# A third pair of score blocks on VectorE in every second head group of an attention kernel

## The chip, the cores and the metric

The kernel runs on one core of a Trainium2 chip. The metric is the device time of one execution in microseconds (us), lower is better. Each kernel was run several times next to the kernel before, on the same chip. A profile shows one execution. Its engines are PE (TensorE; PEld is its weight loads), ACT (ScalarE), DVE (VectorE), POOL (GpSimd) and SP (the queue that issues most transfers, 541 of 601). The granted clock is the share of its full clock that TensorE was given. "L497" is line 497 of the kernel's file; the changed kernel has one line more, so lines after 513 are one higher there.

## The reference, cut to what matters

```python
def _A_ref(x, wqkv, wo):                      # x: 1 x 2048 x 512, 32 heads of 16
    q, k, v = split(x @ wqkv)
    scores = einsum("bhqd,bhkd->bhqk", q, k) * Dh ** -0.5
    p = softmax(scores)                       # 32 x 2048 x 2048 exponentials
    return einsum("bhqk,bhkd->bhqd", p, v) -> heads joined @ wo
def _B_ref(q, k, v, shift_k, ssm_k, ssm_D):   # a causal convolution of length 2048 per channel, 512 channels
    ...
return concatenate([a, b], axis=-1)
```

The 134 million exponentials of the softmax are the part that matters. The convolution runs in the background: its matmuls fill PE's time between the attention's, and 268 MB of shifted filter rows (tile WR) are loaded for it.

## The kernel before

The scores come in blocks of 128 keys x 512 queries. A head group (four heads, 512 queries) has 64 blocks. There are 32 groups, 0 to 31; groups 4 to 31 are the steady part. PE works in steps of three blocks, 21.3 steps to a group:

```python
for T in range(NT + 3):          # NT = 692 steps
    emit_qk(T)                   # PE: 3 score matmuls into 3 PSUM banks; ACT: one exponential over them
    emit_pv(...)                 # PE: weighted sums of blocks whose exponentials are done
    emit_bg(T)                   # PE: a slice of the convolution or of a projection, through PSUM bank 7
    if dve_fill and (bank_free == before or dve_fill[0][0] <= T):
        dve_fill.pop(0)[1]()     # DVE: one piece of a pair's exponential
    ...                          # DVE: pieces that end a group (transposes, division)
```

Two sets of three PSUM banks alternate, so the score matmuls of step T+2 overwrite the banks of step T and wait until these have been read (in the trace before, 304 waits for ACT's reading, 119.7 us). DVE and ACT work through their queues in order: in the trace before all DVE operations (804) and all 698 operations of ACT start in the order of the program, compared by line and tile. PE takes the matmuls of a step in the order of the loop above as well (score matmuls, weighted sums, background; seen step by step in the trace before from 400 to 417 us, where in one step two background matmuls stand among the weighted sums), so a score matmul that waits for its bank holds up what follows it.

Exponentials are split between two engines. In most steps ACT takes all three blocks, 1536 columns. In four steps of a group the third block goes to DVE and ACT takes 1024 columns. DVE does two such blocks together, a pair, with bit arithmetic and a polynomial:

```python
DVE_AT = ((3, 5), (12, 14))      # two pairs in each group: the steps that hand over their third block
DVE_LAG = 8

def exp_on_dve(b, bank, h, T):   # shortened
    # "conversion": reads the PSUM bank and so frees it for the score matmuls of step T + 2
    h_fix[i] = dve.op(tensor_scalar(EI[:, i % 2, :], PS[:, bank, :], FIX_LO, FIX_ADD, max, add),
                      [h, h_pair.get(p - 1)])
    def split():                 # mantissa to EM, power of two to EI
        dve.op(tensor_scalar(EM, EI, 0x7fffff, 0x3f800000, and, or))
        dve.op(tensor_scalar(EI, EI, 0x7f800000, 0x40000000, and, xor))
    def horner(j):               # EH = (EH + B) * m, three times; polynomial of degree 4 in m
        dve.op(scalar_tensor_tensor(EH, src, (B3, B2, B1)[j], m, add, mult))
    def last():                  # PTD = (EH + B0) * power of two
        dve.op(scalar_tensor_tensor(PTD, EH, B0, EI, add, mult))
    if i % 2:                    # after the second block of the pair
        dve_fill.extend([split, horner 0, horner 1, horner 2, last])   # one piece a step, as above
```

DVE also evacuates the background's results from bank 7 (YB, QN, QT, OUTA), and PE's next background matmul waits for that.

The softmax here doesn't subtract the row's maximum and nothing guards it: scores larger than these inputs give would overflow.

Of the kernel before, what the change touches and what calls it, by code (L numbers as in the profile page):

```python
# [6 lines left out]
ALU = mybir.AluOpType  # L7
BF16 = mybir.dt.bfloat16
FP32 = mybir.dt.float32
INT32 = mybir.dt.int32  # L10
# [5 lines left out]
QB = 512  # L16
NQB = S // QB
# [9 lines left out]
LKZ = PAD + S  # L27
R_W = 12
R_PT = 4
R_O = 16  # L30
R_A = 4
CHB = 32
PVB = 6
# [8 lines left out]
B0, B1, B2, B3 = 37.6797618003151, 23.053950042922654, 12.310574509367148, -0.15702561410827162  # L42
OCT = 2.0 ** 23
QSCALE = SCALE * math.log2(math.e) * OCT
FIX_LO = -118.0 * OCT
FIX_ADD = (math.log2(C4) - 1.0) * OCT
DVE_AT = ((3, 5), (12, 14))
DVE_LAG = 8
PACE = 3.9

# [43 lines left out]
def bass_concat_heads__mha_block__ssm_conv_h3__prompt_kernel(  # L94
# [17 lines left out]
    def enter(cm):  # L112
        ctxs.append(cm)
        return cm.__enter__()

    def sem(name):
        return enter(nc.semaphore(name))

    def sb(name, shape, dt=BF16):
        return enter(nc.sbuf_tensor(name, shape, dt))  # L120
# [11 lines left out]
    WKV = sb("WKV", [128, 2, 4, D])  # L132
    OTN = sb("OTN", [128, R_O, QB])
    DT = sb("DT", [128, QB], FP32)
# [4 lines left out]
    IDN = sb("IDN", [128, 128])  # L139
    SHK = sb("SHK", [128, 4, 4])  # L140
    PTD = sb("PTD", [128, 2, QB])
    EI = sb("EI", [128, 2, QB], INT32)
    EM = sb("EM", [128, 2, QB], INT32)
    EH = sb("EH", [128, 2, QB], FP32)
    JNK = sb("JNK", [128, 2], FP32)
# [15 lines left out]
    PS = enter(nc.psum_tensor("PS", [128, 8, 512], FP32))  # L161


    pe, act, dve, pool, sp = [Eng(sem(n)) for n in ("s_pe", "s_act", "s_dve", "s_pool", "s_sp")]
# [191 lines left out]
    def unit(u, bank, eng=None):  # L356
        if u[0] == "x":
            turn_x(u[1], u[2], bank, dve)
        elif u[0] == "t":
            spread_tap(u[1], bank)  # L360
        else:
            evac_unit(u, bank, pe_unit(u, bank), eng)
# [65 lines left out]
    chunks = []  # L428
    b_ = 0
    while b_ < NBLK:  # L430
        T = len(chunks)
        n = 2 if (T % 2 == 1 and T < N_EARLY) else 3
        n = min(n, NBLK - b_)
        chunks.append((list(range(b_, b_ + n)), [3 * (T % 2) + i for i in range(n)]))
        b_ += n
    NT = len(chunks)
# [29 lines left out]
    dve_pv = {}  # L466
    for n in range(2, NQB * NG):
        t0 = chunk_of[first[n]][0]
        if t0 < N_EARLY + 30:
            continue  # L470
        for pair in DVE_AT:
            for t in pair:
                on_dve[chunks[t0 + t][0][2]] = len(on_dve)
                dve_pv[chunks[t0 + t][0][2]] = t0 + pair[1] + DVE_LAG

    h_exp = {}
    h_blk = {}
# [28 lines left out]
    h_fix = {}  # L506
    h_ptd = {}
    h_pair = {}

    def exp_on_dve(b, bank, h, T):  # L510
        i = on_dve[b]
        p = i // 2
        m = EM[:, :, :].bitcast(FP32)
        st = {}
        h_fix[i] = dve.op(lambda e: e.tensor_scalar(EI[:, i % 2, :], PS[:, bank, :], FIX_LO, FIX_ADD, ALU.max, ALU.add),  # L515
                          [h, h_pair.get(p - 1)])

        def split():
            st["m"] = dve.op(lambda e: e.tensor_scalar(EM[:, :, :], EI[:, :, :], 0x7fffff, 0x3f800000,  # L519
                                                       ALU.bitwise_and, ALU.bitwise_or), [h_fix[i], h_fix[i - 1]])  # L520
            st["e"] = dve.op(lambda e: e.tensor_scalar(EI[:, :, :], EI[:, :, :], 0x7f800000, 0x40000000,  # L521
                                                       ALU.bitwise_and, ALU.bitwise_xor), [st["m"]])

        def horner(j):
            src = m if j == 0 else EH[:, :, :]
            st["h"] = dve.op(lambda e: e.scalar_tensor_tensor(EH[:, :, :], src, (B3, B2, B1)[j], m, ALU.add, ALU.mult),  # L526
                             [st["m"], st.get("h")])

        def last():
            h_pair[p] = h_blk[b] = h_blk[b1] = dve.op(  # L530
                lambda e: e.scalar_tensor_tensor(PTD[:, :, :], EH[:, :, :], B0, EI[:, :, :].bitcast(FP32),  # L531
                                                 ALU.add, ALU.mult), [st["h"], st["e"], h_ptd.get(p - 1)])
        if i % 2:
            b1 = blk_on_dve[i - 1]
            dve_fill.extend(zip(range(T + DVE_LAG - 6, T + DVE_LAG - 1),
                                [split, lambda: horner(0), lambda: horner(1), lambda: horner(2), last]))
        return h_fix[i]
# [2 lines left out]
    dve_fill = []  # L540

    def oslot(n):
        return (n + 12) % R_O

    h_otn = {}
    dve_later = []
# [31 lines left out]
    def finish_group(n, h, T):  # L578
# [16 lines left out]
        def turn_back(i0, i1):  # L595
            sl = slice(128 * i0, 128 * i1)
            h_otn[(n, i1)] = h_otn[n] = dve.op(
                lambda e: e.transpose(out=OTN[:, oslot(n), sl], in_=dtn[:, sl]),  # L598
                [st["h"], h_wqp[7]] + ([h_op[((n - R_O) // NG, t)] for t in range(4)] if n >= R_O else []))
        if last:  # L600
# [56 lines left out]
    def load_wr(d):  # L657
        r = d % R_W
        deps = [h_kzw[0], h_kvc[0]] if d < R_W else [h_wrfree[d - R_W]]
        src = bass.AP(tensor=kz_ap.tensor, offset=kz_ap[d, 0].offset, ap=[[1, 128], [1, S]])  # L660
        h_wr[d] = dma(sp, d_wr[r], WR[:, r, :], src, deps)

    def load_qn(i, deps):
        h_qn[i] = dma(pool, d_q[i % 2], QN[:, i % 2, :, :],
                      q2[:, 128 * i:128 * i + 128].rearrange("(t p) d -> p t d", p=128), deps)
# [70 lines left out]
    def now(T):  # L736
        t1 = N_EARLY + 30
        return 12.0 + 1.36 * min(T, t1) + 1.28 * max(T - t1, 0)

    def group_step(qb, g):  # L740
        return NT * (qb * NG + g) // (NQB * NG)

    def unit_job(u):
        return [lambda: pe_unit(u, BGB, (0, 1)), lambda: evac_unit(u, BGB, pe_unit(u, BGB, (2, 3)))]
# [5 lines left out]
    def start_job(job):  # L750
        state["gap"] += 1
        state["job"] = job
        state["job"].pop(0)()

    def emit_bg(T):
        st = state
        if not kv_pieces and not st["started"]:
            st["started"] = True
            st["dma"] = now(T) + 18.0
            for i in range(R_W // 4):  # L760
                st["wr"].append(st["dma"] + 1.5)
            for d in range(R_W):
                load_wr(d)
            for i in range(2):
                load_qn(i, [h_kvc[0], h_kzt[0]])
        if T <= max(early):
            if T in early:
                unit(early[T], 5 if T < N_EARLY - 1 else 7)
            return
        if T == max(early) + 1:  # L770
            load_wop(pe_last())
        if st["turn"]:
            conv_turn(st["qd"] // 8 - 1)
            st["turn"] = False
            st["gap"] = 0
            return
        if not st["started"]:
            return
        st["lags"] = min(st["lags"] + PACE, 4.0 * LAGS)
        if st["job"]:  # L780
            st["job"].pop(0)()
            return
        if st["qd"] % 4 == 0 and st["lag"] == 0:
            ready = st["qd"] < C // 4 and st["wr"][st["qd"]] <= now(T)
            jobs = []
            if st["op"] < len(later_op) and (later_op[st["op"]][0] * NG + NG - 1) in h_otn:
                u = later_op[st["op"]]
                jobs.append((NT * (u[0] + 2) // NQB, "op", op_job, u))
            if st["q"] < len(later_q) and T >= group_step(later_q[st["q"]][1] - 2, later_q[st["q"]][2]) + 30:
                u = later_q[st["q"]]  # L790
                jobs.append((group_step(u[1], u[2]), "q", lambda *u: unit_job(u), u))
            if jobs:
                due, kind, make, u = min(jobs, key=lambda j: j[0])
                if st["gap"] < 1 or T + 60 > due or not ready:
                    start_job(make(*u))
                    st[kind] += 1
                    return
        left = min(LAGS, int(st["lags"]))
        while left and st["qd"] < C // 4 and st["wr"][st["qd"]] <= now(T) and not st["turn"]:
            n0 = st["lag"]  # L800
            n1 = min(n0 + left, NB)
            left -= n1 - n0
            st["lags"] -= n1 - n0
            conv_lags(st["qd"], n0, n1)
            st["lag"] = n1 % NB
            if n1 == NB:
                st["qd"] += 1
                for i in range(4):
                    st["dma"] = max(st["dma"], now(T) + 3.0) + 1.42
                st["wr"].append(st["dma"] + 1.5)  # L810
                if st["qd"] % 4 == 0:
                    st["gap"] = 0
                    st["turn"] = st["qd"] % 8 == 0
                    break

    def pe_last():
        return (pe.sem, pe.n)
# [3 lines left out]
    for b in range(NBLK):  # L821
        qb, g, kt, s = blk(b)
        n = qb * NG + g
        t = dve_pv[b] if b in on_dve else chunk_of[b][0] + 2
        if n >= 2:
            t = max(t, chunk_of[last_blk[n - 1]][0] + 3)
# [31 lines left out]
    for t in range(4):  # L858
        h = op_mm(qb, t, 7, 8, banks[t])
# [55 lines left out]
```

## Time and profile before

| | kernel before |
|---|---|
| time, median of the first 3 runs | 926.25 us |
| span of the profiled run | 927.0 us |
| busy: ACT, PE, DVE | 96%, 81%, 68% |
| exponentials on ACT | 552 of 1536 columns, 140 of 1024 |
| blocks on DVE | 112 (28 groups x 4) |

The first view is the page's part 1, busy time of each engine with its share of the span, and part 4, the chain of waits that ended last.

```profile
...
PE 748.9 (81%) x12846; PEld 337.1 (36%) x12892; DVE 634.9 (68%) x804; ACT 892.2 (96%) x699; POOL 47.0 (5%) x65
...
ACT 67%; PE 16%; DMA 7%; DVE 7%; issue 1%; SPq 1%; ACTq 0%
...
```

ACT is the limit: 96% busy and 67% of the chain.

The groups of instructions by form (line, engine, operation, tiles, shapes, count | busy us, mean ns of one | idle time before them and what ended it) give the costs. First ACT:

```profile
...
L497 ACT ACTIVATE PT<-PS 128x1536 bf16<-128x1536 f32 x552 | 788.6, 1632 | 13.9 <-PE PS L490 13.1
L497 ACT ACTIVATE PT<-PS 128x1024 bf16<-128x1024 f32 x140 | 163.8, 1170 | 3.4 <-PE PS L490 3.4
...
```

These durations overlap, so a mean of 1632 ns is not what one costs. From start to start the median is 1.331 us for the long form and 0.904 us for the short one. A block of 512 columns is therefore worth 0.427 us of ACT, 0.834 ns per column. With these two pitches the exponentials of a group in the steady part take 26.72 us on average; I call that the pure time. Groups 4 to 31 took 27.89 us each, 1.17 us more. I call that the excess.

Then the operations of a pair on DVE:

```profile
...
L526 DVE SCALAR_TENSOR_TENSOR EH<-EH,EM 128x1024 f32<-128x1024 f32 x112 | 142.1, 1269 | 3.4
L515 DVE TENSOR_SCALAR EI<-PS 128x512 int32<-128x512 f32 x112 | 78.6, 702 | 90.8 <-PE PS L490 89.9
L526 DVE SCALAR_TENSOR_TENSOR EH<-EM 128x1024 f32<-128x1024 f32 x56 | 71.3, 1273 | 0.0
L531 DVE SCALAR_TENSOR_TENSOR PTD<-EH,EI 128x1024 bf16<-128x1024 f32 x56 | 69.9, 1248 | 1.8
L519 DVE TENSOR_SCALAR EM<-EI 128x1024 int32<-128x1024 int32 x56 | 40.2, 717 | 1.6
L521 DVE TENSOR_SCALAR EI<-EI 128x1024 int32<-128x1024 int32 x56 | 39.8, 710 | 1.9
...
```

A pair is two of L515 and one each of L519 and L521, three of L526 and one of L531: about 7.8 us, once overlaps are taken off.

Waits (who waited for whom: us in all, times, longest):

```profile
...
DVE EI L515 <- PE PS L490: 89.9, 88, 3.1
...
ACT PT L497 <- PE PS L490: 16.5, 34, 2.4
...
```

DVE waits 90 us for scores to convert, so it is ahead, and ACT waits only 16.5 us for scores. No wait of the score matmuls for the conversion is in the list.

The last view is the timeline of DVE alone (start us, duration us, instruction, and in brackets the idle time before it) in group 9, an odd group, whose first pair runs here:

```profile
...
277.63 0.67 DVE L515 TENSOR_SCALAR EI<-PS 128x512 int32<-128x512 f32 x1
...
279.78 0.70 DVE L515 TENSOR_SCALAR EI<-PS 128x512 int32<-128x512 f32 x1
...
283.11 2.70 DVE L526 SCALAR_TENSOR_TENSOR EH<-EH,EM 128x1024 f32<-128x1024 f32 x2
285.85 1.23 DVE L531 SCALAR_TENSOR_TENSOR PTD<-EH,EI 128x1024 bf16<-128x1024 f32 x1
...
288.78 0.69 DVE L515 TENSOR_SCALAR EI<-PS 128x512 int32<-128x512 f32 x1 [0.25 <-PE PS L490]
...
291.79 0.88 DVE L515 TENSOR_SCALAR EI<-PS 128x512 int32<-128x512 f32 x1
...
```

The first pair is finished at 287.1, and the next conversion, at 288.78, finds DVE idle, waiting for PE.

### The profile page before, as it was taken

What the parts mean: (1) busy time and instruction counts of PE and PEld (TensorE: products, weight loads), DVE (VectorE), ACT (ScalarE), POOL (GpSimd) and SP (SyncE); (2) the same over time, 40 slices, a digit from 0 to 9 for tenths busy, and PEclk for the clock granted to TensorE, in tenths of its full rate; (3) what the DMA queues carried; (4) which work ended last, traced back from release to release, by engine and by line L of the source; (5) the groups of instructions that cost most, each with busy time, mean ns of one, the idle gap of its engine ahead of it and who ended that gap; (6) DMA issues with size and microseconds to landing.
All of it is one profiled execution on the core that took longest, in us unless ns stands there. A gap on an engine that the chain in (4) does not pass through costs nothing.

```text
span 927.0 us, 28312 instructions
## 1 busy us (share of the span) xinstructions
PE 748.9 (81%) x12846; PEld 337.1 (36%) x12892; DVE 634.9 (68%) x804; ACT 892.2 (96%) x699; POOL 47.0 (5%) x65
## 2 busy tenths in 40 slices
PE   7998787887777878877777778888778877778887
PEld 3332233433333433333343333333334333333432
DVE  4789627767667756677676577677677677667764
ACT  5999999999999999999999899999999999999995
POOL 2113130000000100000000000000000000000000
PEclk9999999999999999999999899999999999999987
DMA  9643569999999999989999999996999999997741
GB/s 312 232 143 114 155 227 393 335 382 354 373 337 384 362 368 373 341 329 352 386 361 368 330 392 334 353 344 238 375 394 348 394 336 385 346 377 317 297 166 46
DMA packets 88570, 295.59 MB, mean 319 GB/s; under 512 B 11269, under 2 KB 19458, under 8 KB 88066
## 3 DMA queue, kind: packets, MB, share of 16 engines
q1 hardware_dynamic: 82114, 280.13, 81.0%
q0 software_dynamic: 3936, 12.58, 4.2%
q8 instruction: 102, 1.67, 0.7%
q10 hardware_dynamic: 2400, 1.05, 0.4%
q14 instruction: 18, 0.15, 0.0%
HBM read 287.31 MB, written 6.42 MB: 317 GB/s over the span
## 4 chain that ended last, share of the span: by engine, by line
ACT 67%; PE 16%; DMA 7%; DVE 7%; issue 1%; SPq 1%; ACTq 0%
ACT PT L497 67%; DMA WR<-kz_scratch 6%; PE PS L490 4%; PE PS L562 3%; PE PS L678 3%; PE PS L630 2%; PE PS L310 1%; SPq L171 1%; DMA WKV<-in_A_wqkv_dram 1%; PE PS L296 1%; DVE WR L374 1%; DVE WR L378 1%; PE PS L303 1%; DVE EH L526 1%; DVE KTo L333 1%
## 5 line engine op out<-in xcount | busy, mean ns | idle before, releaser
L497 ACT ACTIVATE PT<-PS 128x1536 bf16<-128x1536 f32 (+1 forms) x692 | 886.9, 1539 | 17.3 <-PE PS L490 16.5
L490 PE MATMUL PS<-QT,KTo 32*128 32x512 bf16 x2048 | 277.0, 394 | 128.8 <-ACT PT L497 119.7
L678 PE MATMUL PS<-WR,KV 128*2 128x128 bf16 (+15 forms) x8192 | 306.3, 228 | 18.6 <-DMA WR<-kz_scratch 12.3
L562 PE MATMUL PS<-PT,VAF 128*32 128x512 bf16 x1936 | 295.1, 399 | 2.1 <-DVE DT L584 1.3
L678 PEld LDWEIGHTS PS<-WR,KV 128*14 128x14 bf16 (+15 forms) x8192 | 195.8, 107 | 52.4 <-issue 36.4
L490 PEld LDWEIGHTS PS<-QT,KTo 32*128 32x128 bf16 x2048 | 67.6, 91 | 291.4 <-ACT PT L497 241.0
L526 DVE SCALAR_TENSOR_TENSOR EH<-EH,EM 128x1024 f32<-128x1024 f32 x112 | 142.1, 1269 | 3.4
L515 DVE TENSOR_SCALAR EI<-PS 128x512 int32<-128x512 f32 x112 | 78.6, 702 | 90.8 <-PE PS L490 89.9
L562 PEld LDWEIGHTS PS<-PT,VAF 128*32 128x32 bf16 x1936 | 69.0, 93 | 151.6 <-issue 140.1
L584 DVE STREAM_TRANSPOSE DT<-PS 128x512 f32<-128x512 f32 x31 | 22.2, 717 | 100.1 <-PE PS L562 100.1
L526 DVE SCALAR_TENSOR_TENSOR EH<-EM 128x1024 f32<-128x1024 f32 x56 | 71.3, 1273 | 0.0
L531 DVE SCALAR_TENSOR_TENSOR PTD<-EH,EI 128x1024 bf16<-128x1024 f32 x56 | 69.9, 1248 | 1.8
L519 DVE TENSOR_SCALAR EM<-EI 128x1024 int32<-128x1024 int32 x56 | 40.2, 717 | 1.6
L521 DVE TENSOR_SCALAR EI<-EI 128x1024 int32<-128x1024 int32 x56 | 39.8, 710 | 1.9
L296 PE MATMUL PS<-xT,WQP 128*128 128x512 bf16 x105 | 32.1, 382 | 9.6 <-DVE QN L714 3.2
L630 PE MATMUL PS<-WKV,OTN 128*128 128x512 bf16 x117 | 32.6, 389 | 3.6 <-DVE YB L694 1.2
L324 DVE TENSOR_SCALAR QT<-PS 128x512 bf16<-128x512 f32 x32 | 22.1, 690 | 19.5 <-PE PS L296 19.5
L694 DVE CAST YB<-PS 128x512 bf16<-128x512 f32 x32 | 21.9, 685 | 14.6 <-PE PS L562 12.5
L562 PE MATMUL PS<-PTD,VAF 128*32 128x512 bf16 x112 | 23.5, 417 | 3.4 <-DVE PTD L531 3.3
L171 POOL DMA_DIRECT2D out_dram<-QN x4 | 4.7, 1179 | 405.9 <-DVE QN L714 405.9
L598 DVE STREAM_TRANSPOSE OTN<-DTN 128x512 bf16<-128x512 bf16 (+1 forms) x35 | 23.0, 664 | 0.7
L171 POOL DMA_DIRECT2D out_dram<-OUTA x12 | 6.6, 550 | 332.6 <-DVE OUTA L638 309.8
(62 smaller groups left out, 262.8 us busy)
## 6 DMA issues: line engine op xcount, KB each, us to landing
WR<-kz_scratch SPq DMA_DIRECT2D x512, 512.0 KB, 8.2
WR<-in_B_k_dram POOLq DMA_DIRECT2D x16, 256.0 KB, 4.5
kz_scratch<-WR SPq DMA_DIRECT2D x1, 2176.0 KB, 9.0
KV<-in_A_x_dram SPq DMA_DIRECT2D x4, 512.0 KB, 6.7
QN<-in_B_q_dram POOLq DMA_DIRECT2D x4, 512.0 KB, 11.0
out_dram<-QN POOLq DMA_DIRECT2D x4, 512.0 KB, 8.4
WR<-in_B_v_dram SPq DMA_DIRECT2D x6, 256.0 KB, 2.7
QT<-in_B_k_dram POOLq DMA_DIRECT2D x6, 256.0 KB, 4.8
```

What stands on the lines that cost most here:

```text
L296: return e.matmul(PS[:, bank, :], lhsT=WQP[:, dc, g, :], rhs=xT[:, dc, qb * 512:(qb + 1) * 512], start=(dc == 0), stop=(dc == 3))
L490: ins = e.matmul(PS[:, bank, :], lhsT=KTo[32 * s:32 * s + 32, g // 2, kt * 128:(kt + 1) * 128], rhs=QT[32 * s:32 * s + 32, qb % 2, g, :], ...
L497: h_exp[T] = act.op(lambda e: e.activation(PT[:, T % R_PT, 0:n * QB], PS[:, banks[0]:banks[0] + n, :].rearrange("p b f -> p (b f)"), ACT.E ...
L515: h_fix[i] = dve.op(lambda e: e.tensor_scalar(EI[:, i % 2, :], PS[:, bank, :], FIX_LO, FIX_ADD, ALU.max, ALU.add), [h, h_pair.get(p - 1)])
L519: st["m"] = dve.op(lambda e: e.tensor_scalar(EM[:, :, :], EI[:, :, :], 0x7fffff, 0x3f800000, ALU.bitwise_and, ALU.bitwise_or), [h_fix[i], ...
L521: st["e"] = dve.op(lambda e: e.tensor_scalar(EI[:, :, :], EI[:, :, :], 0x7f800000, 0x40000000, ALU.bitwise_and, ALU.bitwise_xor), [st["m"]])
L526: st["h"] = dve.op(lambda e: e.scalar_tensor_tensor(EH[:, :, :], src, (B3, B2, B1)[j], m, ALU.add, ALU.mult), [st["m"], st.get("h")])
L531: lambda e: e.scalar_tensor_tensor(PTD[:, :, :], EH[:, :, :], B0, EI[:, :, :].bitcast(FP32), ALU.add, ALU.mult), [st["h"], st["e"], h_ptd. ...
L562: ins = e.matmul(PS[32 * s:32 * s + 32, pvb(qb * NG + g), :], lhsT=VAF[:, kt, h * VW:h * VW + 32], rhs=rhs, start=(kt == 0), stop=(kt == K ...
L598: lambda e: e.transpose(out=OTN[:, oslot(n), sl], in_=dtn[:, sl]),
L630: ins = e.matmul(PS[:, bank, :], lhsT=OTN[:, oslot(qb * NG + g), t * 128:(t + 1) * 128], rhs=WOP[:, g, :], start=(g == 0), stop=(g == NG - 1))
L678: ins = e.matmul(PS[32 * c:32 * c + NB - n, BGB, 128 * (kk % 4):128 * (kk % 4) + 128], lhsT=KV[:, n:NB, d], rhs=WR[:, d % R_W, 128 * (NB - ...
```

## The change

Its intent: DVE has time left (68% busy), ACT has none. In every odd group three pairs are handed over in place of two. As the pairs now follow closely, the integer tile EI holds two pairs. Its SBUF comes from the projection input tile OTN, cut from 16 slots to 12, and for that the output projections must be done earlier.

```diff
-R_O = 16
+R_O = 12
-DVE_AT = ((3, 5), (12, 14))
+DVE_AT = (((3, 5), (12, 14)), ((2, 3), (7, 9), (13, 15)))
-    EI = sb("EI", [128, 2, QB], INT32)
+    EI = sb("EI", [128, 2, 2, QB], INT32)
-        for pair in DVE_AT:
+        for pair in DVE_AT[n % 2]:
...
-                dve_pv[chunks[t0 + t][0][2]] = t0 + pair[1] + DVE_LAG
+                dve_pv[chunks[t0 + t][0][2]] = t0 + min(pair[1] + DVE_LAG, 22)
...      # in exp_on_dve: the conversion waits for the pair before the last one
-        h_fix[i] = dve.op(lambda e: e.tensor_scalar(EI[:, i % 2, :], PS[:, bank, :], FIX_LO, FIX_ADD, ALU.max, ALU.add),
-                          [h, h_pair.get(p - 1)])
+        h_fix[i] = dve.op(lambda e: e.tensor_scalar(EI[:, p % 2, i % 2, :], PS[:, bank, :], FIX_LO, FIX_ADD, ALU.max, ALU.add),
+                          [h, h_pair.get(p - 2)])
...
-        return (n + 12) % R_O
+        return (n + 4) % R_O
...      # output projections are due earlier
-                jobs.append((NT * (u[0] + 2) // NQB, "op", op_job, u))
+                jobs.append((group_step(u[0] + 1, 2 + u[1] // 2), "op", op_job, u))
```

More of the change, by code (lines that the diff above doesn't have):

```diff
@@ L513, in exp_on_dve @@
         m = EM[:, :, :].bitcast(FP32)
+        ei = EI[:, p % 2, :, :]
         st = {}
-        h_fix[i] = dve.op(lambda e: e.tensor_scalar(EI[:, i % 2, :], PS[:, bank, :], FIX_LO, FIX_ADD, ALU.max, ALU.add),
-                          [h, h_pair.get(p - 1)])
+        h_fix[i] = dve.op(lambda e: e.tensor_scalar(EI[:, p % 2, i % 2, :], PS[:, bank, :], FIX_LO, FIX_ADD, ALU.max, ALU.add),
+                          [h, h_pair.get(p - 2)])
         def split():
-            st["m"] = dve.op(lambda e: e.tensor_scalar(EM[:, :, :], EI[:, :, :], 0x7fffff, 0x3f800000,
-                                                       ALU.bitwise_and, ALU.bitwise_or), [h_fix[i], h_fix[i - 1]])
-            st["e"] = dve.op(lambda e: e.tensor_scalar(EI[:, :, :], EI[:, :, :], 0x7f800000, 0x40000000,
+            st["m"] = dve.op(lambda e: e.tensor_scalar(EM[:, :, :], ei, 0x7fffff, 0x3f800000,
+                                                       ALU.bitwise_and, ALU.bitwise_or), [h_fix[i], h_fix[i - 1], h_pair.get(p - 1)])
+            st["e"] = dve.op(lambda e: e.tensor_scalar(ei, ei, 0x7f800000, 0x40000000,
                                                        ALU.bitwise_and, ALU.bitwise_xor), [st["m"]])
@@ L530, in last @@
             h_pair[p] = h_blk[b] = h_blk[b1] = dve.op(
-                lambda e: e.scalar_tensor_tensor(PTD[:, :, :], EH[:, :, :], B0, EI[:, :, :].bitcast(FP32),
+                lambda e: e.scalar_tensor_tensor(PTD[:, :, :], EH[:, :, :], B0, ei.bitcast(FP32),
                                                  ALU.add, ALU.mult), [st["h"], st["e"], h_ptd.get(p - 1)])
```

## The prediction

> **What bounds it now.** ScalarE. The page has ACT busy 892 of 927 us (96%), the chain of waits is 67% exponentials (line 497), and from 120 us to the end the stretches have ACT 97 to 100% busy. Groups by form: 552 exponentials of 1536 columns and 140 of 1024. In the time order one costs 1.331 us or 0.904 us from start to start when nothing holds it, so a 512-column block is worth 0.427 us[...]. 28 head groups of 21.3 steps need 26.7 us of ACT each and take about 28.0.
>
> **What the change removes.** 14 of the 28 groups hand over six blocks in place of four: 28 blocks x 0.427 = 12 us off ScalarE.
>
> **What it adds.** VectorE. One pair costs two conversions out of PSUM (0.66 to 0.70), two bit splits (0.70 + 0.63), three Horner steps (1.25 to 1.3 each) and the last product (1.25): 7.8 us. 14 pairs are 110 us: busy from 635 to about 745 us. It lands unevenly: a group has about 4 us of other VectorE work (transposes, projection, convolution evacuations), so an even group stays at 20 us of 28 and an odd one comes to 27.5 us, against 25.8 us of exponentials. In odd groups VectorE becomes the longer engine, and it runs in order.
>
> **How much reaches the critical path.** The conversion frees the PSUM bank, and the score matmuls two steps later need that bank. From the transpose at the group's start to the conversion of step 15, VectorE has about 20 us of work (three transposition ops 2, two whole pairs 15.6, two conversions 1.3, evacuations 1.2), and ScalarE's steps in that time are 15.2 us; with what may be late, about 18. So the conversions at steps 9, 13 and 15 are late, by 1.5 to 2.5 us in all per odd group, against 0.85 us gained: +9 to +23 us over 14 groups. Part hides under stalls already there (about 33 us beyond the pure exponentials since 120 us: loads of WR, PE jobs). DMA is 0.94 to 0.99 busy in most stretches, but loads land at up to one per 1.37 us against a mean of 1.53, so it follows. The second integer buffer and the projection slots cost little.
>
> **Prediction.** 931 us, about +0.5%; 8 in 10 between 915 and 948. Faster by over 2%: 0.03; within 2%: 0.84; slower by over 2%: 0.13.
>
> **What would show it.** ACT busy down by about 12 us, with 524 long exponentials and 168 short ones. VectorE 740 to 750 us. In the waits, score matmuls and their weight loads waiting for VectorE's conversion (line 515 before), which does not appear now; VectorE's own idle time before that conversion (90 us) much smaller; ScalarE idle for scores up from 16.5 us. Odd groups no shorter than even ones.
>
> **What would make it wrong.** If the late conversions are hidden better than I think (PE running ahead more, the pair's work slipping into the tail of the odd group and the next even group), most of the 12 us is kept: 915 to 920. If an evacuation in VectorE's queue, waiting for PE, now blocks a pair that PE itself waits for, as at 504 to 514 us of this trace, the stalls multiply and each also delays the next WR loads: 945 or more.

The 0.427 us is the difference of two measured pitches, 1.331 and 0.904 us, and the forecast remains the 926 us of the kernel before and about 5 us more, 931 us. That VectorE "runs in order" is what the trace before shows for its 804 operations.

## The result, and the profile after

| | before | after |
|---|---|---|
| time, median | 927.66 us (4 runs) | 950.97 us (4 runs, 947.44 to 951.73) |
| ratio | | 1.0243, 95% interval 1.0208 to 1.0278 |
| span of the profiled run | 927.0 us | 948.9 us |
| mean length of an even group, 4 to 30 | 27.89 us | 27.61 us |
| mean length of an odd group, 5 to 31 | 27.89 us | 29.34 us |
| its pure exponentials | 26.72 us | 25.86 us |
| its DVE busy time | 19.6 us | 26.1 us |

Ratios here and below are the mean time of one kernel's fast runs over that of the other's fast runs of the same rounds, so they are not quite the ratio of the medians that are quoted. A group's length runs from the start of its first exponential in the trace to the start of the next group's first.

The kernel became 2.4% slower. The spans differ by 21.8 us: the 14 odd groups give +20.2, the 14 even ones -3.9, the part before group 4 +2.6 and the end +2.9.

The page's parts 1 and 4, ACT's forms, and the conversion's group, of the changed kernel:

```profile
...
PE 758.5 (80%) x12849; PEld 339.9 (36%) x12892; DVE 730.5 (77%) x916; ACT 885.9 (93%) x699; POOL 47.7 (5%) x65
...
ACT 52%; DVE 26%; PE 17%; DMA 2%; issue 2%; ACTq 0%; SPq 0%; DVEq 0%
...
```

```profile
...
L497 ACT ACTIVATE PT<-PS 128x1536 bf16<-128x1536 f32 x524 | 747.4, 1591 | 33.0 <-PE PS L490 32.1
L497 ACT ACTIVATE PT<-PS 128x1024 bf16<-128x1024 f32 x168 | 188.5, 1145 | 9.6 <-PE PS L490 8.4
...
```

```profile
...
L516 DVE TENSOR_SCALAR EI<-PS 128x512 int32<-128x512 f32 x140 | 98.2, 701 | 63.5 <-PE PS L490 62.7
...
```

ACT has 28 long exponentials fewer and 28 short ones more, as planned. By the two pitches that is 12 us less work, and the page's busy time falls by 6 us. ACT's share of the chain falls from 67% to 52%, and DVE's rises from 7% to 26%.

The waits:

```profile
...
DVE EI L516 <- PE PS L490: 62.7, 53, 4.2
...
ACT PT L497 <- PE PS L490: 40.5, 75, 1.9
...
PE PS L490 <- DVE EI L516: 20.1, 23, 1.8
...
```

The third line shown is new: 20.1 us in which score matmuls wait for a conversion to free their bank. ACT's own wait for scores rises from 16.5 to 40.5 us, and DVE's wait for scores falls from 90 to 63 us. All waits of PE for DVE together, from 135 us to the end, rise from 20.9 to 49.4 us: 20.1 for the conversion, 10.0 in place of 4.4 for the evacuation YB, the rest for PTD, QT, QN and others.

Group 9 shows how. The stretches (busy us of PE, PEld, DVE, ACT and POOL with counts, granted clock, share of DMA, GB/s), first before, then after:

```profile
...
274.20:301.00 26.80, 20.89 (x433) 9.99 (x434) 20.14 (x23) 26.80 (x22) 0.00 (x0) 1.00 0.95 355
...
```

```profile
...
280.30:309.30 29.00, 23.84 (x402) 10.34 (x400) 26.72 (x32) 26.84 (x23) 2.15 (x3) 1.00 0.53 193
...
```

The granted clock is 1.00 in both. The group lasts 29.0 us in place of 26.8 us, although ACT's pure time is 0.85 us less. DVE is busy 26.7 us, and ACT idles for 2.2 us. The DVE timeline of that group, cut:

```profile
...
283.15 0.69 DVE L516 TENSOR_SCALAR EI<-PS 128x512 int32<-128x512 f32 x1 [1.25 <-PE PS L490]
...
284.54 0.69 DVE L516 TENSOR_SCALAR EI<-PS 128x512 int32<-128x512 f32 x1
...
290.59 0.82 DVE L516 TENSOR_SCALAR EI<-PS 128x512 int32<-128x512 f32 x1
291.33 2.47 DVE L527 SCALAR_TENSOR_TENSOR EH<-EH,EM 128x1024 f32<-128x1024 f32 x2
293.72 0.77 DVE L516 TENSOR_SCALAR EI<-PS 128x512 int32<-128x512 f32 x1
294.38 1.23 DVE L532 SCALAR_TENSOR_TENSOR PTD<-EH,EI 128x1024 bf16<-128x1024 f32 x1
...
298.42 1.27 DVE L527 SCALAR_TENSOR_TENSOR EH<-EH,EM 128x1024 f32<-128x1024 f32 x1
299.61 0.68 DVE L516 TENSOR_SCALAR EI<-PS 128x512 int32<-128x512 f32 x1
300.21 1.22 DVE L527 SCALAR_TENSOR_TENSOR EH<-EH,EM 128x1024 f32<-128x1024 f32 x1
301.47 1.23 DVE L532 SCALAR_TENSOR_TENSOR PTD<-EH,EI 128x1024 bf16<-128x1024 f32 x1
302.61 0.68 DVE L516 TENSOR_SCALAR EI<-PS 128x512 int32<-128x512 f32 x1
...
```

From 286 us on the view lists no wait of DVE in this cut. The conversions (L516) at 293.72, 299.61 and 302.61 stand behind Horner steps and products (L527, L532) of the pairs in front. PE and ACT at the same time, same view:

```profile
...
300.44 0.39 PE L490 MATMUL PS<-QT,KTo 32*128 32x512 bf16 x3 [0.94 <-DVE EI L516]
...
300.88 2.38 ACT L497 ACTIVATE PT<-PS 128x1024 bf16<-128x1024 f32 x2 [0.18 <-PE PS L490]
...
303.44 0.39 PE L490 MATMUL PS<-QT,KTo 32*128 32x512 bf16 x3 [1.19 <-DVE EI L516]
...
303.88 2.89 ACT L497 ACTIVATE PT<-PS 128x1536 bf16<-128x1536 f32 x2 [0.62 <-PE PS L490]
...
```

The scores at 300.44 start 0.15 us after the conversion of 299.61 has ended, and those at 303.44 the same way after that of 302.61. Each time ACT runs dry and waits: 0.18 and 0.62 us.

Over all 14 odd groups, the conversion ends this long after the end of its own scores:

| step (odd group) | 2 | 3 | 7 | 9 | 13 | 15 |
|---|---|---|---|---|---|---|
| after, us | 0.82 | 0.93 | 2.31 | 1.54 | 1.73 | 1.69 |

In the kernel before, the four steps are at 0.76 to 1.07 us.

Where ACT loses the time can be read from the starts of its exponentials. The delay of a step is the time from the start of its exponential to the start of the next one, less the pitch of its form. Summed over a stretch of steps, on average for one odd group:

| steps of the odd group | 0 to 6 | 7 to 11 | 12 to the end |
|---|---|---|---|
| before, us | 0.41 | 0.23 | 0.52 |
| after, us | 0.91 | 1.74 | 0.80 |

Most of the new delay, 1.5 of 2.3 us, comes in steps 7 to 11, at and behind the conversions of steps 7 and 9. Steps 12 to the end, where those of 13 and 15 count, add 0.3 us. The 0.5 us in steps 0 to 6 is taken up under e6 and e8.

### The profile page after: what moved, and what is told of

It reads as the page before. It is cut to its first block, busy times and chain, and to the rows that moved or that the text cites. A ratio compares the mean times of both kernels' runs of the same rounds, so it can differ in the third digit from the quotient of the medians.

```text
span 948.9 us, 28416 instructions
## 1 busy us (share of the span) xinstructions
PE 758.5 (80%) x12849; PEld 339.9 (36%) x12892; DVE 730.5 (77%) x916; ACT 885.9 (93%) x699; POOL 47.7 (5%) x65
## 4 chain that ended last, share of the span: by engine, by line
ACT 52%; DVE 26%; PE 17%; DMA 2%; issue 2%; ACTq 0%; SPq 0%; DVEq 0%
ACT PT L497 52%; DVE EH L527 8%; PE PS L490 5%; PE PS L563 4%; DVE EI L516 3%; PE PS L631 3%; DVE PTD L532 2%; PE PS L679 2%; DVE EM L520 2%; DVE EI L522 2%; PE PS L310 2%; DMA WR<-kz_scratch 1%; PE PS L296 1%; DMA WKV<-in_A_wqkv_dram 1%; DVE OTN L599 1%
## 5 line engine op out<-in xcount | busy, mean ns | idle before, releaser
L497 ACT ACTIVATE PT<-PS 128x1536 bf16<-128x1536 f32 (+1 forms) x692 | 880.6, 1483 | 42.6 <-PE PS L490 40.5
L679 PE MATMUL PS<-WR,KV 128*9 128x128 bf16 (+15 forms) x8192 | 312.7, 228 | 12.8 <-DVE QT L324 5.4
L679 PEld LDWEIGHTS PS<-WR,KV 128*9 128x9 bf16 (+15 forms) x8192 | 198.7, 107 | 45.1 <-issue 28.1
L527 DVE SCALAR_TENSOR_TENSOR EH<-EH,EM 128x1024 f32<-128x1024 f32 x140 | 175.0, 1250 | 4.0
L516 DVE TENSOR_SCALAR EI<-PS 128x512 int32<-128x512 f32 x140 | 98.2, 701 | 63.5 <-PE PS L490 62.7
L527 DVE SCALAR_TENSOR_TENSOR EH<-EM 128x1024 f32<-128x1024 f32 x70 | 88.8, 1268 | 0.0
L532 DVE SCALAR_TENSOR_TENSOR PTD<-EH,EI 128x1024 bf16<-128x1024 f32 x70 | 86.8, 1240 | 1.5
L520 DVE TENSOR_SCALAR EM<-EI 128x1024 int32<-128x1024 int32 x70 | 50.2, 717 | 2.3
L522 DVE TENSOR_SCALAR EI<-EI 128x1024 int32<-128x1024 int32 x70 | 49.9, 713 | 2.4
L563 PE MATMUL PS<-PTD,VAF 128*32 128x512 bf16 x140 | 30.0, 425 | 5.1 <-DVE PTD L532 5.0
L695 DVE CAST YB<-PS 128x512 bf16<-128x512 f32 x32 | 21.8, 682 | 9.1 <-PE PS L563 5.7
L599 DVE STREAM_TRANSPOSE OTN<-DTN 128x512 bf16<-128x512 bf16 (+1 forms) x35 | 23.1, 666 | 0.4
```

What stands on the lines that cost most here:

```text
L497: h_exp[T] = act.op(lambda e: e.activation(PT[:, T % R_PT, 0:n * QB], PS[:, banks[0]:banks[0] + n, :].rearrange("p b f -> p (b f)"), ACT.E ...
L516: h_fix[i] = dve.op(lambda e: e.tensor_scalar(EI[:, p % 2, i % 2, :], PS[:, bank, :], FIX_LO, FIX_ADD, ALU.max, ALU.add), [h, h_pair.get(p ...
L520: st["m"] = dve.op(lambda e: e.tensor_scalar(EM[:, :, :], ei, 0x7fffff, 0x3f800000, ALU.bitwise_and, ALU.bitwise_or), [h_fix[i], h_fix[i - ...
L522: st["e"] = dve.op(lambda e: e.tensor_scalar(ei, ei, 0x7f800000, 0x40000000, ALU.bitwise_and, ALU.bitwise_xor), [st["m"]])
L527: st["h"] = dve.op(lambda e: e.scalar_tensor_tensor(EH[:, :, :], src, (B3, B2, B1)[j], m, ALU.add, ALU.mult), [st["m"], st.get("h")])
L532: lambda e: e.scalar_tensor_tensor(PTD[:, :, :], EH[:, :, :], B0, ei.bitcast(FP32), ALU.add, ALU.mult), [st["h"], st["e"], h_ptd.get(p - 1)])
```

## The experiments

Theory A: DVE works its queue in order; in an odd group of the changed kernel its work up to the last conversions is longer than ACT's steps, conversions and evacuations come late, and PE and then ACT wait. (The deadline of a conversion is the score matmul two steps later, which needs its bank.) Rival 1: the other parts of the change (slots, earlier projections) cost the time. Rival 2, called theory B in some texts: short exponentials in close order leave PE too little time, so the saving on ACT cannot be had at all. "Excess" is a group's length less its pure exponentials.

**e1_two_pairs: everything but the third pair.**

```diff
-DVE_AT = (((3, 5), (12, 14)), ((2, 3), (7, 9), (13, 15)))
+DVE_AT = (((3, 5), (12, 14)), ((3, 5), (12, 14)))
```

> The changed kernel with everything but the third pair: two integer buffers, twelve projection slots and earlier output projections stay, and every group hands over two pairs as before. Theory (VectorE's queue is too long in odd groups and the conversions out of PSUM come late): 925 to 931 us, odd and even groups alike near 27.9 us. Rival 1 (the slots and the moved output projections cost the time): 940 us or more with the excess in both kinds of group.

Measured: 927.55 us, ratio 0.9991 (0.9936 to 1.0045). Excess 0.80 us in even and 1.33 us in odd groups. Rival 1 falls: slots, buffers and moved projections cost nothing that shows.

**e2_cubic: one Horner step less.**

```diff
-C4 = 0.013534167911703966
-B0, B1, B2, B3 = 37.6797618003151, 23.053950042922654, 12.310574509367148, -0.15702561410827162
+C4 = 0.07802455204645152
+B0, B1, B2 = 5.794770457783116, 6.12336457770677, -0.10261477111778086
...
-                                [split, lambda: horner(0), lambda: horner(1), lambda: horner(2), last]))
+                                [split, lambda: horner(0), lambda: horner(1), last]))
```

The coefficients are a fit of degree 3 to 2^(m-1) on 1 to 2, with a largest relative error of 0.00007.

> The changed kernel with a polynomial of degree 3 in place of 4, so one Horner step (1.25 to 1.3 us) less per pair; the same blocks are handed over, the exponentials on ScalarE are the same 524 long and 168 short. VectorE's busy time in an odd group falls from 26.1 to about 22.4 us, under the 25.9 us of exponentials. Theory: the odd groups' excess over the pure exponentials falls from 3.5 us to 1.2 to 2.0 us, the score matmuls' waits for the conversion nearly vanish, time 918 to 930 us. Rival 2 (short exponentials in close order leave PE too little time, so that the saving of ScalarE cannot be had at all): odd groups stay near 29.3 us, time 940 us or more.

Measured: 935.41 us, ratio 1.0085 (1.0015 to 1.0154), correct. Odd excess 2.61 us in place of 3.47, DVE busy 23.0 us. It helped, and by more than rival 2 allows, but by less than I expected, and score matmuls still wait 16.9 us for conversions (20.1 after). The conversion of step 7 was still 2.40 us behind its scores: it stands behind a transpose of the group before, both splits and one or two Horner steps of the first pair, and in 7 of the 14 groups the pair's product too, so a sum over the group is not the test; the sum in front of each conversion is.

**e3_cubic_before: the control.** The same edit in the kernel before.

> Control: the kernel before with the same degree 3. Theory: VectorE was not the limit there, so 922 to 928 us, within 0.6% of before. If it falls by 10 us or more, VectorE's work was already on the critical path everywhere and the lateness in odd groups is not special.

Measured: 927.25 us, ratio 0.9977 (0.9921 to 1.0032). With two pairs per group, DVE's work is not on the critical path, as expected.

**e6_extra_work: the load without the saving.** The pair at (7, 9) stays on ACT; DVE does its eight operations (the text on record says seven) on other data.

```diff
+                if pair == (7, 9):
+                    twice.add(chunks[t0 + t][0][2])
+                else:
+                    dve_pv[chunks[t0 + t][0][2]] = t0 + min(pair[1] + DVE_LAG, 22)
...
-        n = len(bl) - (bl[-1] in on_dve)
+        n = len(bl) - (bl[-1] in dve_pv)
...      # the conversion of such a block reads SBUF, holds no bank, and nobody reads its product
+        elif bl[-1] in twice:
+            exp_on_dve(bl[-1], banks[-1], h_wqp[7], T)
```

> The changed kernel in which the middle pair of an odd group is computed twice: ScalarE keeps its two blocks (all exponentials there long, so 552 long and 140 short as before) and VectorE does a pair's seven operations on other data, holding no PSUM bank and read by nobody. It adds a load on VectorE and takes nothing off ScalarE. Theory: the load alone delays the real conversions; odd groups grow from 27.9 to 28.7 to 30 us, time 938 to 957 us. Rival 2 (short exponentials in close order): odd groups as before, 926 to 931 us.

Measured: 943.34 us, ratio 1.0154 (1.0099 to 1.0209), correct. Odd groups last 29.07 us, with 25.6 us of DVE busy. ACT's forms and the waits:

```profile
...
L501 ACT ACTIVATE PT<-PS 128x1536 bf16<-128x1536 f32 x552 | 780.5, 1590 | 20.6 <-PE PS L494 19.9
L501 ACT ACTIVATE PT<-PS 128x1024 bf16<-128x1024 f32 x140 | 156.7, 1147 | 6.5 <-PE PS L494 6.2
...
```

```profile
...
ACT PT L501 <- PE PS L494: 26.1, 58, 1.4
...
PE PS L494 <- DVE EI L522: 8.2, 11, 1.3
...
```

The kernel takes 1.5% longer, with as few short exponentials as before. But e6 is not a clean test against rival 2: two of its short exponentials, at steps 2 and 3, are adjacent, which none were before. Its odd groups have 1.16 us more delay than before. Of this, 0.53 us lies in steps 0 to 6, mostly in front of the added work; e8 below has 0.46 us there with a light load on DVE. Only the other 0.63 us can be put down to the added load.

**e8_no_horner: the saving without most of the load.** The result is wrong (relative error 0.16).

```diff
-                lambda e: e.scalar_tensor_tensor(PTD[:, :, :], EH[:, :, :], B0, ei.bitcast(FP32),
+                lambda e: e.scalar_tensor_tensor(PTD[:, :, :], m, B0, ei.bitcast(FP32),
...
-                                [split, lambda: horner(0), lambda: horner(1), lambda: horner(2), last]))
+                                [split, last], [0] * 1 + [r]))   # r: not before the pair in front was read
...
-        if dve_fill and (bank_free == before or dve_fill[0][0] <= T):
+        if dve_fill and dve_fill[0][2] <= T and (bank_free == before or dve_fill[0][0] <= T):
```

> Wrong result on purpose: the changed kernel with its three pairs at the same steps, without any of the Horner steps, so that a pair costs VectorE two conversions, two splits and one product (about 4 us in place of 7.8), in even groups too. ScalarE's exponentials, the places of the short ones and PE's matmuls are those of the changed kernel. Theory A: odd excess near 1.2 us, time 915 to 922. Theory B: odd excess stays at 2 us or more, 930 or more.

Measured: 920.75 us, ratio 0.9912 (0.9866 to 0.9959). In the profiled run (914.87 us, the fastest of its four) odd groups last 27.44 us, excess 1.57 us. PE's waits:

```profile
...
PE PS L490 <- ACT PT L497: 125.0, 320, 0.6
...
PE PS L490 <- ACT KTo L331: 0.8, 1, 0.8
...
```

There is no wait for the conversion in this list any more. So most of the saving can be had with the same short exponentials in the same places. A rest of rival 2 is true: the delay of ACT in the step after the two adjacent short exponentials, (2, 3), is 0.37 us on average here, 0.40 us in the changed kernel and in e6, and 0.11 us after step 3 in the kernel before.

**e7_cubic_spread: degree 3, other places.**

```diff
+DVE_AT = (((3, 5), (12, 14)), ((3, 5), (8, 10), (13, 15)))     # and degree 3 as in e2
```

> Degree 3 as in e2, with the odd group's pairs moved from steps (2,3), (7,9), (13,15) to (3,5), (8,10), (13,15). In e2 the conversion of step 7 was still 2.40 us behind its scores, since it queues behind the group's transposes and the first pair. Theory A (VectorE's work, in the order of its queue): the conversions are spread and the work fits, odd excess from 2.6 us to 1.2 to 2.0 us, time 919 to 930. Theory B (what costs is the handing over itself, short exponentials leaving PE too little time): as many short exponentials as in e2, excess stays at 2.3 us or more, 932 to 938.

Measured: 925.39 us, ratio 0.9978 (0.9929 to 1.0026). The time is in the range of theory A, but the odd excess, 2.28 us in the profiled run (932.09 us, the slowest of its four), is above it. Conversions were still 2.24 us behind at step 13. The theory is half met.

**e9_spread: degree 4, the same places as e7.**

> The changed kernel with degree 4 and the odd group's pairs at (3,5), (8,10), (13,15), the places alone. If crowding at the start of the group is what costs, it should gain: 938 to 945. If the amount of work up to the conversion of step 15 is what costs, later first pairs only leave VectorE less time for the same work before step 15: 948 to 960.

Measured: 962.92 us, ratio 1.0388 (1.0341 to 1.0436), slower than the changed kernel. The conversions of steps 10, 13 and 15 were 2.01, 2.59 and 2.22 us behind. Starting the first pair later leaves less time for the same work before step 15: the second reading, and more strongly than I thought. Part of the loss is in the even groups that follow (28.71 us in place of 27.61 after), in the profiled run (970.37 us, the slowest of its four, granted clock 0.935; the others had 0.949 to 0.952, against 0.967 to 0.980 of the kernel before).

e7 and e9 differ in the degree alone and ran in the same rounds: one Horner step less in each pair takes 37.5 us off, with the same short exponentials at the same steps, none of them adjacent. Together with e3, where the same edit brings nothing, this is the clearest evidence for theory A, and it speaks against rival 2 as the main cause.

**e10_cubic_all_spread: degree 3, three pairs in every group, places as e7.**

> Degree 3 and three pairs, spread, in every group, odd and even. Theory A: VectorE has 22 to 23 us of work in each group, under the 25.9 us of exponentials, but little to spare; 912 to 928. Theory B: every group has the excess that odd groups have in e2, 28.5 us each: 940 or more.

Measured: 928.67 us, ratio 0.9990 (0.9941 to 1.0040). Excess 2.10 us in even and 1.86 us in odd groups. The 24 us that ACT is spared go back into waits: PE waits 51.3 us for DVE. Theory A's range ended at 928, so this is a near miss.

**e13_every_fourth: half the dose.**

```diff
-        for pair in DVE_AT[n % 2]:
+        for pair in DVE_AT[n % 4 == 1]:
```

> The changed kernel with the third pair only in groups 5, 9, 13 and so on to 29: 7 groups in place of 14, and not in the last group. Theory (each group with three pairs of degree 4 pays for itself alone): these 7 groups last 29.0 to 29.6 us, the others 27.4 to 28.0; 934 to 940 us, about half of the loss. If the loss came from the end of the kernel or from something that the whole run shares, the time would not halve: under 931 or over 945.

Measured: 937.06 us, ratio 1.0095 (1.0051 to 1.0140). The 7 groups last 29.62 us on average (26.87 to 31.21), the others 27.70. The loss is 0.95% where the changed kernel lost 2.43%, a little under half. The end after the last exponential took 10.9 us, as before (10.9) and not as after (13.8): the last group, 31, no longer has a third pair. That accounts for the 3 us at the end; e2, where group 31 has a third pair of degree 3, is at 10.9 us as well.

**e4_places: the middle pair at (9, 10).**

```diff
+DVE_AT = (((3, 5), (12, 14)), ((2, 3), (9, 10), (13, 15)))     # degree 4
```

> The changed kernel, degree 4, with the odd group's middle pair at (9,10) in place of (7,9). The work before the conversion of step 15 is the same, so most of the loss stays; but the conversion that came 2.3 us late at step 7 now comes at step 9, with the first pair done. Odd excess 2.5 to 3.3 us in place of 3.5; 936 to 948 us.

Measured: 956.96 us, ratio 1.0315 (1.0279 to 1.0351). A miss: slower than the changed kernel. The conversion of step 15 is now 2.33 us behind (1.69 after) and that of step 13 2.22 (1.73). What the middle pair gained by coming later, the third lost: ACT's delays in odd groups are 1.11 us in steps 7 to 11 (1.74 after) and 1.59 us from step 12 on (0.80).

**e12_cubic_all_2: degree 3, every group, places (2,3), (9,10), (13,15).**

> Degree 3 and three pairs in every group at (2,3), (9,10), (13,15), where e10 had (3,5), (8,10), (13,15). More of VectorE's work comes early, so the conversions of steps 13 and 15, 2.05 to 2.35 and 1.6 us behind their scores in e10, come less late: excess 1.4 to 1.9 us per group, 912 to 924 us.

Measured: 932.86 us, ratio 1.0065 (1.0000 to 1.0130). Another miss: conversions were less late than in e10 (1.86 to 1.92 and 1.31 to 1.36 us at steps 13 and 15), yet the time was not better. ACT's delay after the adjacent pair (2,3) is back (0.30 and 0.35 us per group), and this profiled run had a granted clock of 0.953 where that of e10 had 0.978. How much each of the two takes was not separated.

**e11_quad_all: degree 2, three pairs in every group.**

```diff
-C4 = 0.013534167911703966
-B0, B1, B2, B3 = 37.6797618003151, 23.053950042922654, 12.310574509367148, -0.15702561410827162
+C4 = 0.33718971771810213
+B0, B1 = 2.0204581964752233, -0.04965416335465768
-DVE_AT = (((3, 5), (12, 14)), ((2, 3), (7, 9), (13, 15)))
+DVE_AT = (((3, 5), (8, 10), (13, 15)), ((3, 5), (8, 10), (13, 15)))
...
-                                [split, lambda: horner(0), lambda: horner(1), lambda: horner(2), last]))
+                                [split, lambda: horner(0), last], [0] * 2 + [r]))
```

The last entry is the condition of e8, which keeps the product from being written before the pair in front was read; e12 has it too.

> Degree 2 (largest relative error of the polynomial 0.0017) and three pairs, (3,5), (8,10), (13,15), in every group: VectorE has about 19.5 us of work in each group and ScalarE 25.9 us. Theory: excess 1.2 to 1.6 us in every group, conversions hardly late, 905 to 915 us, faster than both kernels.

Measured: 905.92 us (905.22 to 906.72), ratio 0.9769 (0.9741 to 0.9798), correct. This beats both kernels. The excess is 0.74 us in even and 1.58 us in odd groups, and the conversions of steps 8 to 15 end 0.80 to 1.66 us behind their scores. The page and the waits:

```profile
...
PE 749.1 (83%) x12892; PEld 334.6 (37%) x12892; DVE 635.4 (70%) x860; ACT 869.0 (96%) x699; POOL 46.9 (5%) x65
...
ACT 70%; PE 16%; DVE 7%; DMA 5%; issue 1%; SPq 1%; ACTq 0%
...
```

```profile
...
ACT PT L497 <- PE PS L490: 16.9, 36, 2.2
...
PE PS L490 <- DVE EI L516: 6.1, 13, 0.8
...
```

DVE is as busy as in the kernel before (635 us) with 168 blocks in place of 112. ACT waits for scores as little as before (16.9 us). DVE is cheaper per block, so more blocks fit in front of each conversion's deadline. The price is a coarser exponential.

The runs side by side (odd groups; PE's waits for DVE from 135 us on, in the profiled run; the kernel before took 927.66 to 928.94 us in the rounds of these runs):

| run | pairs, degree | DVE busy in an odd group | PE waits for DVE | time |
|---|---|---|---|---|
| before | 2, 4 | 19.6 us | 20.9 us | 927.66 |
| e1 | 2, 4 | 19.7 | 17.5 | 927.55 |
| e3 | 2, 3 | 17.2 | 15.3 | 927.25 |
| after | 3, 4 | 26.1 | 49.4 | 950.97 |
| e6 | 2 and one unused, 4 | 25.6 | 39.9 | 943.34 |
| e9 | 3, 4, spread | 25.6 | 62.2 | 962.92 |
| e4 | 3, 4, middle pair at (9, 10) | 26.0 | 51.4 | 956.96 |
| e13 | 3 in every second odd group, 4 | 22.9 | 28.0 | 937.06 |
| e2 | 3, 3 | 23.0 | 36.2 | 935.41 |
| e7 | 3, 3, spread | 22.9 | 28.2 | 925.39 |
| e10 | 3 in all groups, 3, spread | 23.1 | 51.3 | 928.67 |
| e12 | 3 in all groups, 3, other steps | 23.1 | 38.8 | 932.86 |
| e8 | 3, none | 16.0 | 11.1 | 920.75 |
| e11 | 3 in all groups, 2 | 19.5 | 15.2 | 905.92 |

## Why the prediction was wrong

The measured 951 us lie above the range of 915 to 948; the direction, a loss and not a gain, was right.

- "12 us off ScalarE": right. 28 long exponentials became short ones.
- "an odd one comes to 27.5 us, against 25.8 us of exponentials": right in kind; DVE was busy 26.1 us in an odd group, ACT's pure time was 25.86 us.
- "the conversions at steps 9, 13 and 15 are late, by 1.5 to 2.5 us in all per odd group": right in size, in part by luck. The odd excess rose from 1.17 to 3.47 us, by 2.30. But the latest conversion was that of step 7, which I had not named; 1.5 us of the rise came in steps 7 to 11, 0.3 us from step 12 on, and 0.5 us in steps 0 to 6, where e8 shows nearly the same (0.46 us) with a light load on DVE.
- "+9 to +23 us over 14 groups": right, near the upper end. The odd groups gave +20.2 us.
- "Part hides under stalls already there (about 33 us ...)": this is the step that failed. It turned +9 to +23 us into +5 us, a discount of some 11 us from the middle of that range, and no such discount came. In the kernel before, the 33 us are spread over the groups: 0.4 to 1.3 us in those with full clock, 1.76 us on average in the 12 of 28 groups in which the PE clock was halved for a time (last section). In steps 7 to 11 of an odd group, where most of the new delay came, there were 0.23 us of stalls to hide it under. In groups with full clock throughout, the odd excess was 0.73 us before (8 groups) and 3.24 us after (5 groups): +2.51 us, the upper end of the forecast lateness with nothing taken off. Even groups gave 0.28 us each back, 3.9 us in all.
- Not foreseen: the end (+2.9 us), since the last group is odd and its third product comes last; e13 shows it. The +2.6 us before group 4, where no third pair exists yet, I put down to scatter; group 4 starts at 137.8 us there, and at 134.8 to 137.0 us in the other runs.
- "The second integer buffer and the projection slots cost little": right, by e1.
- "It [DMA] follows": right. PE's waits for WR loads fell from 12.3 to 4.4 us. (The 1.37 us per load was too slow: in the trace before, the median distance of two landings is 1.28 us.)

The prediction also named a way to "945 or more": an evacuation in DVE's queue waits for PE and blocks a pair, and the WR loads come later. The time came, this mechanism did not. From the start of an odd group to the exponential of step 17, DVE's idle time in front of evacuations (QT, QN, YB, OUTA) was 1.03 us per group before and 1.16 us after, and the waits for WR loads fell.

The signs that the prediction named came as follows. ACT's busy time fell by 6 us, not 12: an exponential after a gap is not overlapped by the one before and counts with its whole length, 1.49 us on average for the long form where the pitch is 1.331, and from group 4 on there were 51 such long ones after and 21 before; DVE's rose to 730, not 740 to 750. The new wait, the smaller idle time of DVE and the larger one of ACT are all there. Odd groups are not only no shorter but longer than even ones.

With 77% busy over the run, DVE was the limit inside half of the groups, the odd ones, where it was busy for 26.1 us against 25.86 us of pure exponentials. Looking at those groups alone was the right step; taking a discount for stalls elsewhere was the wrong one.

Two things stay open: how much of the loss comes by way of the granted clock (0.96 in the profile after, 0.97 before; the groups with full clock show that most of it does not), and why e12 did no better than e10, beyond what is told there.

## What to carry to other kernels

Before work goes to an engine with idle time, add up what stands in its queue in front of each operation that others wait for, here the read that frees a PSUM bank, and compare that with the time to the deadline; the busy share of the run did not show it here (77%, with the conversion of step 7 ending 2.31 us after its scores). A stall counted in one place is not a discount on a stall in another. Making the moved work cheaper helped: with the third pairs at the same steps, degree 4 lost 3.9% (e9) and degree 3 was level (e7); degree 2, with three pairs in every group, gained 2.3% (e11). Moving it to other steps did not help at degree 4: both sets that were tried were slower.

## The granted clock and the busy shares

- Between 120 and 916 us of the kernel before, the granted clock fell to 0.5 in 13 places, ten times for 3.4 us and three times for 6.8 us; in the changed kernel it did so in 14 places, the longest 10.2 us. In the kernel before, PE was busy 39 to 65% of the 3.4 us in front of each drop, with no single gap over 1.5 us; the other 204 stretches of 3.4 us that stood at full clock and led to no drop, counted in step with the drops, had PE busy 62% or more. In the changed kernel the two ranges overlap more: 30 to 65% in front of a drop, 57% or more elsewhere. There drops followed the stalls as well, for example after 632.3 to 635.7 us with PE busy 1.02 of 3.40 us. Whether the low busy time causes the drop was not tested.
- In the kernel before, groups with a drop had an excess of 1.76 us, groups without one 0.73 us; the difference is more than the cost of the drop alone if the stall that came before the drop lies in the same group. Slower runs of the kernel before tend to have lower clocks: it took 926.18 us at a mean clock of 0.976 and 936.45 us at 0.958. The changed kernel at a clock of 0.975 still took 947.44 us, so the clock is the smaller part of its loss.
- After the change ACT was still the busiest engine (93% against 77% of DVE), and yet the conversions on DVE set the pace in odd groups: score matmuls waited 20.1 us for them. The busy shares did not show it. 68% was harmless and 77% came with a loss of 2.4%, while e10 with 79% (731 us) came out level with the kernel before, since 24 us were taken off ACT.
